# Attention and feed-forward on one core: the scale of x from the sums of squares of v, with a re-dealt instruction order

## The chip, the cores and the metric

The kernel runs on one core of a Trainium2 chip. The metric is device time in microseconds. The program before has a median of 1043.28 us over 3 runs (1041.65 to 1044.36).

## The reference, cut to what matters

```python
# q, k, v: (8 batches, 8 heads, 576 tokens, 64), float32
scores = (1 / sqrt(64)) * q @ k.transpose(0, 1, 3, 2)
scores = where(block_i >= block_j, scores, -1e9)      # blocks of 64 tokens, causal by block
attn = softmax(scores)
x = (attn @ v).transpose(0, 2, 1, 3).reshape(4608, 512)
h = x @ w_in                                          # 512 -> 2048
g = maximum(0.01 * h, h)
out = g @ w_out                                       # 2048 -> 512
```

Every row of `attn` sums to one, so a row of `x` is a weighted mean of rows of `v`.

## The kernel before, in words

**The work.** There are 64 pairs of batch and head ("heads" below) and 19 chunks of tokens, 256 tokens each except two of 128. Attention makes `x` head by head. The feed-forward layer takes a chunk when all eight heads have filled its tokens. Both are interleaved on TensorE, so that feed-forward matmuls (first layer L994, second layer L1012) stand between the attention steps of the later heads.

**One head of attention.** Scores go into the PSUM tile `p_s`: by matmuls in float32 for the first batch and the first part of the second (L586), with split operands `kk` and `qs` for the second and third (L603 and L598), with float16 operands from batch 3 on (L592). VectorE masks (L614) and takes the negated row maximum `nm` (L623). ScalarE takes the exponentials and their sums (L640). Both PSUM banks of `p_s` are used again by the next scores, so these wait until the exponentials have read them. Each head has two rounds: query tiles 0 to 3 (exponentials over 448, 64, 192 and 320 keys), then tile 4 over 576 keys. The sums are inverted (`rec`, L655 to L659). The probabilities are split into a float16 head (L682 on GpSimd, L683 on ScalarE, L684 on VectorE) and the rest (L687 on VectorE). A DMA transposes both (L694); TensorE multiplies them by the split `v` (L813), and L772 to L776 put the result, scaled back, into `x`. The tile of `x` is `xr`, which the profile calls `xr` for even and `slab` for odd batches; `slab` also holds the probabilities.

**Scales.** Operands of float16 matmuls are scaled by powers of two from their size. For `v`, `v_group` loads four heads at a time, takes their squares on ScalarE with an accumulator output (L882, one column of `vn` for each group), sums over partitions by a matmul with ones (L884), halves the exponent (`halved`, L399) and makes the scale and its inverse by integer arithmetic on the exponent (`powers`, L394 and L395). For q and k, `q_group` does the same with 40 squares from batch 3 on (L912, behind the loads `raw<-in_qk` at L911). For `x`, `scale_x` does it for each of ten groups of chunks that become ready together: it squares the tokens of these chunks on ScalarE (L948, a separate instruction for each batch and each half of the channels, 30 in all), adds the columns of `xn` (L958), sums over partitions (L959), and makes the scale `xs` and its inverse `xi`. `split_x` multiplies by `xs` and splits `x` into `xh` and `xl` (L973 to L977); the last layer's output is multiplied by `xi` (L1027).

**The feed-forward layer.** `ffn1` makes `p_h` (L994), ScalarE takes it to `g` (L999), `g` is cast to `gh` (L269 on ScalarE or L270 on VectorE), and the rest `gl` is subtracted on VectorE (L279) or GpSimd (L280). `ffn2` multiplies both by the output weights (L1012).

**What sets the order.** Each step is put into a `Plan` with a rank, what it reads and writes, and one or more engines with a cost for each. `Plan.run` steps through a model of the five engines: an engine that is free takes the ready step of the lowest rank, and a step that several engines can do goes to the first that takes it. The order found this way is written out for each engine, and the engine keeps it. Ranks are positions in units of one head plus an offset for each kind of step (`RL` for loads, `RP`, `RN`, `RV`, `RX` for the steps of a head, `RS` for the scale of `x` and its split, `VD`, `RQ` and `RD` for the groups of v and q). All DMAs stand in one queue, SyncE's.

Of the kernel before, what the change touches and what calls it, by code (L numbers as in the profile page):

```python
# [11 lines left out]
I32 = mybir.dt.int32  # L12
# [3 lines left out]
ALU = mybir.AluOpType  # L16
AX = mybir.AxisListType
# [5 lines left out]
S = 576  # L23
# [14 lines left out]
GROUP = 4  # L38
AHEADV = 3
AHEADQ = 5  # L40
RW = -0.559

RL = 4.551
RP = -0.707
RB = 0.386
RT = 1.718
RV = 2.066
RX = -5.319
RN = -1.998

LEAD = 4.4
LAG = 1.993
RS = 3.252
RG = 0.186
OFF1 = 3.425
OFF2 = -1.79
SL1 = 16.01
AHEAD = 0.432

LAT = 1550  # L60
HOLDP = 521.844
HOLD = 212.637
FILL = 235
FILLTO = 12
# [10 lines left out]
TOP = 204 << 23  # L75
# [2 lines left out]
SLOW = 8000  # L78
SIDE = 34
STEPA = 0.521  # L80
STEPB = 0.346
VD = 4.884
JOINT = 0
SB = 3
RQ = 3.568
RD = 1.25


class Plan:
# [161 lines left out]
def attention_ffn(ctx: ExitStack, tc: tile.TileContext, qk0: bass.AP, qk: bass.AP, v: bass.AP, w_in: bass.AP, w_out: bass.AP, out: bass.AP):  # L251
# [137 lines left out]
    qk16 = [carve(y, [4, S], F16) for y in range(2)]  # L389
    prow = [prow, [carve(1, [pw[t]], F32) for t in range(NT)]]  # L390

    def powers(e, s, i):
        return [
            lambda: nc.vector.tensor_scalar(s().bitcast(I32), e(), -1.0, float(TOP), op0=ALU.mult, op1=ALU.add),  # L394
            lambda: nc.vector.tensor_scalar(i().bitcast(I32), e(), float(BOT), None, op0=ALU.add),  # L395
        ]

    def halved(e, total):
# [541 lines left out]

    def scale_x(e, c0, c1, rank):
        spans_ = list(regions(c0, c1))
        for k, (_, b, o, ln, keys) in enumerate(spans_):

            for y in range(2):

                def square(k=2 * k + y, b=b, o=o, ln=ln, y=y):
                    nc.scalar.activation(  # L948
                        junk[:, : 2 * ln].rearrange("p (a b) -> p a b", a=2), xr[b % 2][:, 2 * y : 2 * y + 2, o : o + ln],
                        AF.Square, accum_out=xn[:, 4 * e + k : 4 * e + k + 1],  # L950
                    )

                near = [x for x in keys if x[2] // 4 == y]
                add([("ACT", act(2 * ln, True) + 190, square)], rank, near, [("xn", e, 2 * k + y), "junk"])
        x = bank()
        num = 2 * len(spans_)
        one = slice(e, e + 1)
        add([("DVE+", 75, lambda: nc.vector.tensor_reduce(xt[:, one], xn[:, 4 * e : 4 * e + num], axis=AX.X, op=ALU.add))], rank, [("xn", e, k) for k in range(num)], [("xt", e)])  # L958
        add([("PE", [(200, lambda: nc.tensor.matmul(p_t[x][:, 0:1], ones, xt[:, one], start=True, stop=True))])], rank, [("xt", e)], [("t", x)])  # L959
        add([("DVE", 68, lambda: halved(xe[:, one], p_t[x][:, 0:1]))], rank, [("t", x)], [("xe", e)])  # L960
        first, second = powers(lambda: xe[:, one], lambda: xs[:, one], lambda: xi[:, one])
        add([("DVE+", 68, first)], rank, [("xe", e)], [("xs", e)])
        add([("DVE+", 68, second)], rank, [("xe", e)], [("xi", e)])
        add([("DVE+", 68, lambda: nc.vector.tensor_mul(xi[:, one], xi[:, one], both))], rank, ["both"], [("xi", e)])
# [80 lines left out]
    for i in range(len(work) + 1):  # L1045
        if i == 0:

            def second(y):
                nc.gpsimd.memset(parts[y], 0.0)

            for y in range(2):
                new = [("ph", y, t, k) for t in (*range(NT), 6) for k in (0, 1)] + [("pt", y, t) for t in (*range(NT), 6)]
                new += [("p", 1, t) for t in range(NT)] + [(a, 1, d) for a in ("xh", "xl") for d in range(0, CH, BLK)] if y else [("x", 1, h, k) for h in range(H) for k in range(3)] + [("ob", 1)]
                new += [("x", y, k, "q") for k in range(4)]
                kind = "wo" if y else "wi"
                add([("POOL", 3300, lambda y=y: second(y))], 0, [("val", bool(y), f) for f in range(NF)], new)
        if i in events:
            here = [c for c in range(NCHUNK) if ready[c] == i]
            at = pos[i]
            nxt = pos[events[events.index(i) + 1]] if i != events[-1] else at + H  # L1060
            num = sum(sizes[c] for c in here) * NU
            done_ = 0
            e = events.index(i)
            scale_x(e, here[0], here[-1] + 1, at + LEAD - RS)
            for c, u in ((c, u) for c in here for u in range(NU)):
                rank = at + LEAD + (nxt - at) * done_ / num
                done_ += sizes[c]
                if u == 0:
                    split_x(c, e, rank - RS)
                ffn1(c, u, rank)  # L1070
                ffn2(c, e, u, rank + (nxt - at) * LAG * sizes[c] / num + 0.003)
        n, kind = work[i + AHEADV] if i + AHEADV < len(work) else (0, "")
        if kind in ("first", "full") and n % GROUP == 0:
            v_group((n - H) // GROUP)
        n, kind = work[i + AHEADQ] if i + AHEADQ < len(work) else (0, "")
        if kind == "full" and n >= SB * H and n % GROUP == 0:
            q_group((n - SB * H) // GROUP)
        if i < len(work):
            attention(i)
# [42 lines left out]
```

## Time and profile before

| | before |
|---|---|
| median of 3 runs | 1043.28 us |
| the profiled execution, whole time | 1045.07 us |
| its span from the first to the last instruction | 1043.3 us |
| TensorE clock granted in it | 1.000 |
| VectorE, ScalarE, GpSimd busy | 719.1, 723.0, 122.7 us |

The profile is of one execution, which took 1045.07 us, 1.79 us (0.17%) over the median of the runs shown; 1.8 us of it lie outside the span. In the views, PE is TensorE's matmuls, PEld its weight loads, DVE VectorE, ACT ScalarE, POOL GpSimd and SPq the queue in which SyncE issues DMAs. Times in the timeline count from the start of the span.

### The profile page before, as it was taken

The page shows a single profiled execution, that of the slowest core. Times are in us where ns is not written, and L with a number is a line of the kernel's source. Part 1 is how long each engine was busy: PE and PEld are TensorE (multiplying, and loading weights), DVE is VectorE, ACT ScalarE, POOL GpSimd, SP SyncE. Part 2 cuts the span into 40 slices and gives each one's busy share as a digit, 9 for nine tenths or more (in the row PEclk, how much of TensorE's full clock was granted, in tenths as well). Part 3 has the DMA queues.
Part 4 walks back from the last instruction along what each step waited for, and adds up shares of the span by engine and source line. Part 5 has one row for each costly group of instructions (what it writes and reads, how often), then busy time and mean ns, then how long its engine had stood idle before and what let it go on. Part 6 is the DMA issues. An engine that isn't in the chain of part 4 may idle for free. (4 is left out here: it accounts for less than half of the span.)

```text
span 1043.3 us, 22412 instructions
## 1 busy us (share of the span) xinstructions
PE 1023.5 (98%) x8496; PEld 740.3 (71%) x8496; DVE 719.1 (69%) x1942; ACT 723.0 (69%) x1692; POOL 122.7 (12%) x168
## 2 busy tenths in 40 slices
PE   9999999998999999999999999999999999999998
PEld 7787767776677777776767777777766777666665
DVE  4787788897888987898787878886666666221111
ACT  5788878778886887887787968786565666322222
POOL 1010122103130111100211101110100001000000
PEclk9999999999999999999999999999999999999999
DMA  7847456996987798989789889986736345100000
GB/s 259 278 164 245 147 137 139 204 195 135 226 183 160 185 219 168 205 188 220 152 167 186 200 189 185 178 184 121 137 92 149 80 98 85 29 1 21 21 1 31
DMA packets 266380, 155.54 MB, mean 149 GB/s; under 512 B 224288, under 2 KB 243232, under 8 KB 266272
## 3 DMA queue, kind: packets, MB, share of 16 engines
q1 hardware_dynamic: 266272, 154.11, 64.6%
q8 instruction: 66, 1.08, 0.4%
q14 instruction: 42, 0.34, 0.1%
HBM read 80.74 MB, written 9.44 MB: 86 GB/s over the span
## 5 line engine op out<-in xcount | busy, mean ns | idle before, releaser
L994 PEld LDWEIGHTS <-wih 128*128 128x128 f16 x2432 | 230.1, 98 | 67.1 <-issue 0.2
L999 ACT ACTIVATE g<-p_h 128x512 f32<-128x512 f32 (+1 forms) x152 | 86.5, 570 | 165.4 <-PE p_h L994 163.3
L994 PE MATMUL p_h<-slab,wih 128*128 128x256 f16 x1152 | 196.4, 273 | 0.0
L279 DVE TENSOR_TENSOR gl<-g,gh 128x512 bf16<-128x512 f32 (+1 forms) x118 | 77.9, 660 | 138.0 <-ACT gh L269 137.4
L1012 PE MATMUL p_o<-woh,gh 128*128 128x512 f16 x576 | 171.4, 379 | 0.0
L1012 PE MATMUL p_o<-wol,gh 128*128 128x512 f16 x576 | 171.3, 379 | 0.0
L1012 PE MATMUL p_o<-woh,gl 128*128 128x512 f16 x576 | 171.3, 379 | 0.0
L1012 PEld LDWEIGHTS <-gh 128*128 128x128 f16 x1152 | 109.7, 99 | 79.0
L994 PE MATMUL p_h<-xh,wih 128*128 128x256 f16 (+1 forms) x640 | 162.0, 262 | 0.0
L994 PE MATMUL p_h<-xh,wil 128*128 128x256 f16 (+1 forms) x640 | 161.9, 262 | 0.0
L994 PE MATMUL p_h<-xl,wih 128*128 128x256 f16 (+1 forms) x640 | 161.9, 262 | 0.0
L994 PE MATMUL p_h<-slab,wil 128*128 128x256 f16 x576 | 157.0, 273 | 0.0
L623 DVE TENSOR_REDUCE nm<-p_s 128x1 f32<-128x192 f32 (+4 forms) x308 | 138.2, 484 | 5.9 <-ACT prow L640 2.5
L994 PEld LDWEIGHTS <-wil 128*128 128x128 f16 x1216 | 118.9, 98 | 12.4
L1012 PEld LDWEIGHTS <-gl 128*128 128x128 bf16 x576 | 56.3, 98 | 67.9
L813 PEld LDWEIGHTS <-vs 128*128 128x128 f16 x1680 | 87.0, 98 | 12.8 <-issue 5.8
L813 PE MATMUL p_t<-slab,vs 128*128 128x128 f16 (+1 forms) x1680 | 90.2, 210 | 5.3 <-DMA slab<-slab 4.4
L687 DVE SCALAR_TENSOR_TENSOR slab<-prow,rec,slab 64x64 f16<-64x64 f32 (+4 forms) x148 | 79.0, 552 | 4.5 <-ACT slab L683 3.7
L687 DVE SCALAR_TENSOR_TENSOR slab<-slab,rec 128x448 f16<-128x448 f32 (+4 forms) x132 | 72.8, 575 | 1.4 <-ACT slab L683 1.0
L269 ACT CAST gh<-g 128x512 f16<-128x512 f32 (+1 forms) x120 | 71.4, 595 | 2.7
L280 POOL TENSOR_TENSOR gl<-g,gh 128x512 bf16<-128x512 f32 (+1 forms) x34 | 41.4, 1219 | 264.1 <-ACT gh L269 177.8
L592 PE MATMUL p_s<-slab 128*128 128x448 f16 (+2 forms) x480 | 67.6, 277 | 1.6 <-ACT prow L640 1.1
(165 smaller groups left out, 1497.7 us busy)
## 6 DMA issues: line engine op xcount, KB each, us to landing
qk_in<-in_qk SPq DMA_DIRECT2D x56, 576.0 KB, 4.9
raw<-in_qk SPq DMA_DIRECT2D x40, 288.0 KB, 3.8
slab<-slab SPq DMA_DIRECT2D x120, 72.0 KB, 4.4
raw<-in_w_in SPq DMA_DIRECT2D x16, 512.0 KB, 5.0
raw<-in_w_out SPq DMA_DIRECT2D x16, 512.0 KB, 4.3
out<-ob SPq DMA_DIRECT2D x19, 256.0 KB, 2.4
v_raw<-in_v SPq DMA_DIRECT2D x7, 640.0 KB, 4.8
raw<-in_v SPq DMA_DIRECT2D x7, 640.0 KB, 5.9
```

The costliest lines, as they stand in the source:

```text
L269: one = lambda: nc.scalar.copy(dst(), src())
L279: ("DVE+" if sb else "DVE", dve(n) + 100, lambda: nc.vector.tensor_sub(dst(), one(), two())),
L280: ("POOL", pool2(n) - (0.25 * n if n == 512 else 0), lambda: nc.gpsimd.tensor_sub(dst(), one(), two())),
L592: go = lambda ap=ap, cols=cols, k0=k0, k1=k1, c=c, first=first, last=last: nc.tensor.matmul(ap, sx1[:, cols], (sx3 if c else sx2)[:, k0:k1 ...
L623: [("DVE", dve(kw[t]), lambda t=t, ap=ap, flat=flat: nc.vector.tensor_reduce(nm[z][: qn[t], t : t + 1], ap[: qn[t]], axis=AX.X if flat els ...
L687: ("DVE+", dve(w) + 62, lambda: nc.vector.scalar_tensor_tensor(part(1), p, by, part(0), op0=ALU.mult, op1=ALU.subtract)),
L813: nc.tensor.matmul(p_t[x][:, c : c + src.free_size()], vs[z][:, (j + 1) % NT], src, start=start, stop=stop)
L994: nc.tensor.matmul(hh[:, i, :n], w[:, f, d, :], x[:, d, :n], start=k == 0, stop=k == len(terms) - 1)
L999: add([("ACT", act(2 * n), lambda: nc.scalar.activation(g[z][:, :, :n], hh[:, :, :n], AF.Prelu, alpha=0.01, scale=DOWN))], rank, [("h", z) ...
L1012: nc.tensor.matmul(p_o[m], a[:, i, m * P : (m + 1) * P], w[:, 2 * u + i, :], start=u == 0 and k == 0, stop=u == NU - 1 and k == 5,)
```

## The change

Two edits come together.

**The scale.** For a group of chunks that holds no token of batch 0, `scale_x` makes no squares of `x` any more. It reduces the columns of `vn` for the v groups of the batches that the chunks touch, and goes on as before, with an exponent that is 15 higher in `powers`, as `x` is kept 2^15 times too large (`UP`). Seven of the ten groups of chunks are such. The three others, two of batch 0 alone and one that spans batches 0 and 1, keep their 8 squares; 22 of the 30 squares and their accumulator reads go. The scale no longer depends on `x`, and its rank is lowered by a further `RX2` = 3.58 heads.

**The order.** Nineteen numbers are changed, which set the ranks and how long GpSimd holds back from a step, and `RX2` is new. The rest of the program is the same, but steps stand elsewhere, and some are on another engine: of the 152 subtractions that make `gl`, 46 are on GpSimd and not 34; GpSimd has 200 rows and not 173, VectorE 40 rows fewer, ScalarE 3 rows fewer. TensorE has the same matmuls in the same number.

```diff
-RS = 3.252
+RS = 3.835
...
-VD = 4.884
+VD = 5.061
...
-RD = 1.25
+RD = 1.347
+RX2 = 3.58
...
-    def powers(e, s, i):
+    def powers(e, s, i, more=0):
         return [
-            lambda: nc.vector.tensor_scalar(s().bitcast(I32), e(), -1.0, float(TOP), op0=ALU.mult, op1=ALU.add),
-            lambda: nc.vector.tensor_scalar(i().bitcast(I32), e(), float(BOT), None, op0=ALU.add),
+            lambda: nc.vector.tensor_scalar(s().bitcast(I32), e(), -1.0, float(TOP - (more << 23)), op0=ALU.mult, op1=ALU.add),
+            lambda: nc.vector.tensor_scalar(i().bitcast(I32), e(), float(BOT + (more << 23)), None, op0=ALU.add),
         ]
...
         spans_ = list(regions(c0, c1))
-        for k, (_, b, o, ln, keys) in enumerate(spans_):
+        b0, b1 = spans_[0][1], spans_[-1][1]
+        groups = range((b0 - 1) * H // GROUP, b1 * H // GROUP)
+        for k, (_, b, o, ln, keys) in enumerate(spans_ if not b0 else ()):
...
-        add([("DVE+", 75, lambda: nc.vector.tensor_reduce(xt[:, one], xn[:, 4 * e : 4 * e + num], axis=AX.X, op=ALU.add))], rank, [("xn", e, k) for k in range(num)], [("xt", e)])
+        each = vn[:, groups[0] : groups[-1] + 1] if b0 else xn[:, 4 * e : 4 * e + num]
+        add([("DVE+", 75, lambda: nc.vector.tensor_reduce(xt[:, one], each, axis=AX.X, op=ALU.add))], rank, [("vn", k) for k in groups] if b0 else [("xn", e, k) for k in range(num)], [("xt", e)])
...
-        first, second = powers(lambda: xe[:, one], lambda: xs[:, one], lambda: xi[:, one])
+        first, second = powers(lambda: xe[:, one], lambda: xs[:, one], lambda: xi[:, one], 15 if b0 else 0)
...
-            scale_x(e, here[0], here[-1] + 1, at + LEAD - RS)
+            scale_x(e, here[0], here[-1] + 1, at + LEAD - RS - (RX2 if begins[here[0]] >= S else 0))
```

Two places on ScalarE show what the order does. Lines of the changed kernel stand 1 further from L395 on, 4 further from L959 on.

**First place: a head of batch 2, whose exponentials of the first round run at 247 us in the trace of before.** `prow` and `slab` hold the probabilities of alternate heads, `junk,xn` is a square of x, `junk,vn` one of v, `junk,ptf` one of q. Before:

```order
L948 ACTIVATE junk,xn<-slab_78 128x768
L882 ACTIVATE junk,vn<-raw 128x1280
L640 ACTIVATE slab_79,sums_104<-p_s,nm_102 128x448
L912 ACTIVATE junk,ptf<-raw 128x576
L640 ACTIVATE slab_79,sums_104<-p_s,nm_102 64x64
L912 ACTIVATE junk,ptf<-raw 128x576
L640 ACTIVATE slab_79,sums_104<-p_s,nm_102 128x192
L912 ACTIVATE junk,ptf<-raw 128x576
L640 ACTIVATE slab_79,sums_104<-p_s,nm_102 128x320
L999 ACTIVATE g_142<-p_h_138 128x512
```

And now, for the same head:

```order
L684 ACTIVATE slab_78<-prow_84,rec_105 128x576
L641 ACTIVATE slab_79,sums_104<-p_s,nm_102 128x448
L641 ACTIVATE slab_79,sums_104<-p_s,nm_102 64x64
L641 ACTIVATE slab_79,sums_104<-p_s,nm_102 128x192
L641 ACTIVATE slab_79,sums_104<-p_s,nm_102 128x320
L1003 ACTIVATE g_141<-p_h_137 128x512
L270 CAST gh_149<-g_141 128x512
```

The square of x is gone, and the squares of v and q no longer stand between the exponentials of this head; they stand around those of the head before it, one v and one q square ahead of its four exponentials, three q squares behind them.

**Second place: a head of batch 4, whose exponential over 576 keys runs at 488 us in the trace of before.** Before:

```order
L272 ACTIVATE slab_78<-qk_in_93,ptf 128x576
L912 ACTIVATE junk,ptf<-raw 128x576
L999 ACTIVATE g_141<-p_h_137 128x512
L272 ACTIVATE slab_78<-qk_in_93,ptf 64x576
L640 ACTIVATE prow_84,sums_103<-p_s,nm_101,ptf 128x576
L948 ACTIVATE junk,xn<-slab_78 128x256
L655 ACTIVATE rec_105<-sums_103 128x1
L948 ACTIVATE junk,xn<-slab_78 128x256
L683 ACTIVATE slab_78<-prow_84,rec_105 128x576
```

And now:

```order
L1003 ACTIVATE g_141<-p_h_137 128x512
L913 ACTIVATE junk,ptf<-raw 128x576
L270 CAST gh_145<-g_141 128x512
L634 ACTIVATE nm_101<-nm_101,ptf 128x1
L273 ACTIVATE slab_78<-qk_in_93,ptf 128x576
L641 ACTIVATE prow_84,sums_103<-p_s,nm_101,ptf 128x576
L656 ACTIVATE rec_105<-sums_103 128x1
L684 ACTIVATE slab_78<-prow_84,rec_105 128x576
```

The two squares of x between the exponential and the split of its result are gone, and the square of q stands four steps ahead of the exponential, where it stood three ahead; one of the two copies of the next head's operands between them is no longer on ScalarE.

## The prediction on record

> **What bounds the kernel now.** The page comes first: who is busy, and which engine the chain that ended last runs over.
>
> ```profile
> PE 1023.5 (98%) x8496; PEld 740.3 (71%) x8496; DVE 719.1 (69%) x1942; ACT 723.0 (69%) x1692; POOL 122.7 (12%) x168
> PE 48%; DVE 0%; ACT 0%; issue 0%
> ```
>
> TensorE bounds the kernel. The change leaves its matmuls alone, so only its idle time can be won: 1043.3 - 1023.5 = 19.8 us. The view of busy time by stage, cut where the idle time changes, shows where that lies (columns: window, its length, then busy time and instructions of PE, PEld, DVE, ACT, POOL; clock; DMA).
>
> ```profile
> 0.00:130.00 130.00, 126.37 (x921) 100.83 (x922) 93.75 (x256) 104.96 (x256) 12.77 (x32) 1.00 0.67 219
> 130.00:240.00 110.00, 107.86 (x860) 76.98 (x859) 94.34 (x256) 85.31 (x207) 19.28 (x24) 1.00 0.75 164
> 240.00:300.00 60.00, 54.89 (x470) 40.66 (x468) 50.76 (x134) 51.51 (x125) 16.44 (x17) 1.00 0.81 181
> 300.00:480.00 180.00, 177.33 (x1657) 129.39 (x1655) 155.51 (x442) 146.14 (x350) 23.75 (x31) 1.00 0.87 189
> 480.00:500.00 20.00, 18.23 (x148) 12.51 (x146) 15.38 (x44) 15.02 (x42) 3.23 (x4) 1.00 0.99 228
> 500.00:560.00 60.00, 59.63 (x531) 43.18 (x529) 49.64 (x140) 47.08 (x109) 10.26 (x14) 1.00 0.85 176
> 560.00:1040.00 480.00, 479.17 (x3925) 336.75 (x3922) 259.69 (x676) 272.96 (x610) 37.01 (x47) 1.00 0.49 101
> ```
>
> PE idles 3.63 us before 130, then 2.14, 5.11, 2.67, 1.77 and 0.37 us up to 560, and 0.83 us in the 480 us after that. TensorE's order is the same in both kernels up to about 130 us, so the first stage stays. What is at stake is the middle: 2.14 + 5.11 + 2.67 + 1.77 + 0.37 = 12.06 us. The list of waits says what PE waited for (total, times, longest):
>
> ```profile
> PE p_t L813 <- DMA slab<-slab: 4.4, 7, 1.9
> PE p_s L603 <- ACT prow L640: 2.4, 2, 1.3
> PE p_s L586 <- ACT rec L655: 1.2, 2, 1.1
> PE p_s L603 <- ACT slab L640: 1.2, 2, 0.6
> PE p_s L592 <- ACT prow L640: 1.1, 2, 0.8
> ```
>
> So PE waits at the attention steps: for the transposed probabilities (4.4 us), and for ScalarE to have read the scores out of PSUM (2.4 + 1.2 + 1.1, and 1.2 us for the first part of batch 1). The list, which goes down to 0.5 us, has no second-layer matmul that waits for `gl`, and no first-layer matmul that waits for a split of x: the scale of x has cover. The change pays, if at all, through ScalarE's load and through the order.
>
> **The squares that go.** The stage view again, for L948 alone (busy us and instructions on ScalarE):
>
> ```profile
> 240.00:300.00 60.00, 2.07 (x4) 1.00 0.81 181
> 300.00:480.00 180.00, 4.03 (x10) 1.00 0.87 189
> 480.00:500.00 20.00, 1.95 (x6) 1.00 0.99 228
> 500.00:560.00 60.00, 0.92 (x2) 1.00 0.85 176
> 560.00:1040.00 480.00, 9.33 (x20) 1.00 0.49 101
> ```
>
> All of these go. The 9.33 us after 560 are worth nothing: PE is dense there, at ScalarE's 272.96 / 480 = 0.57 busy. Before 560 they are 2.07 + 4.03 + 1.95 + 0.92 = 8.97 us.
>
> What is ScalarE's relief worth to PE? The stages themselves give a curve. ScalarE's share against PE's idle share: 51.51/60 = 0.859 with 5.11/60 = 8.5%; 146.14/180 = 0.812 with 1.5%; 47.08/60 = 0.785 with 0.6%; 0.569 with 0.17%. The squares' time taken off, the shares become 0.824, 0.790, 0.769, and 0.654 for the short stage at 480. Read along straight lines between those points, idle becomes 3.3%, 0.8%, 0.6% and 0.35%, or 1.98, 1.39, 0.35 and 0.07 us: it falls by 3.13 + 1.28 + 0.02 + 1.70 = 6.1 us. I leave the stage from 130 to 240 out, since one removed square there is 1 us of 85. This is the upper end.
>
> The lower end is 0: no square of x stands in the chain of the three longest waits. Around 488 us ScalarE's row reads (last column: idle before, and what ended it)
>
> ```profile
> 486.35 0.68 ACT L912 ACTIVATE junk<-raw 128x576 bf16<-128x576 f32 x1 [1.18 <-DMA raw<-in_qk]
> 488.17 0.82 ACT L640 ACTIVATE prow<-p_s,nm,ptf 128x576 f32<-128x576 f32 x1
> 488.98 0.41 ACT L948 ACTIVATE junk<-slab 128x256 bf16<-128x256 f32 x1
> 489.93 0.76 ACT L683 ACTIVATE slab<-prow,rec 128x576 f16<-128x576 f32 x1
> ```
>
> and PE's, with the longest wait of all, at 254 us, as its third row:
>
> ```profile
> 489.13 1.03 PE L592 MATMUL p_s<-slab 128*128 128x448 f16 x8 [0.79 <-ACT prow L640]
> 491.15 1.57 PE L813 MATMUL p_t<-slab,vs 128*128 128x64 f16 x30 [0.99 <-DMA slab<-slab]
> 254.06 1.57 PE L813 MATMUL p_t<-slab,vs 128*128 128x64 f16 x30 [1.88 <-DMA slab<-slab]
> ```
>
> The wait of 0.79 is for an exponential behind a q square, which itself stood 1.18 us waiting for its load; the squares of x come after it. For the transposes, the median from issue to landing and the rows before the wait at 254:
>
> ```profile
> slab<-slab SPq DMA_TRANSPOSE x120, 4.7
> 243.98 0.78 ACT L683 ACTIVATE slab<-prow,rec 128x576 f16<-128x576 f32 x1 [0.30 <-DVE rec L659]
> 244.66 0.83 ACT L948 ACTIVATE junk<-slab 128x768 bf16<-128x768 f32 x1
> 247.87 2.14 SPq L694 DMA_TRANSPOSE slab<-slab  x1
> ```
>
> A transpose that lands at 491.1 was issued near 486.4, ahead of the squares at 488.98; and the one issued at 247.87 belongs to a split that ScalarE ended as the square at 244.66 began. Nor do the curve's stages differ in ScalarE's load alone: the one at 240 holds the subtractions of split operands (L279, L280), which end by batch 3. Between 0 and 6.1 us I take half, 3.0 us.
>
> **The scale's own steps.** Reduction, matmul with ones, exponent and inverse stay, ten times each; for seven of them the rank falls by RX2 = 3.58 heads and by the 0.58 that RS grows. Nothing of PE hangs on them now (no wait in the list above names a split or a scale), so I cost the move at nothing. What hides them is the chunk before, still in the feed-forward; without that cover each would cost about its own chain, a few short instructions.
>
> **The order.** The 12.06 us are dealt again. At 488 us the q square now stands a step further ahead of the exponential, which can give back up to 0.79. At 247 us three q squares and a v square no longer stand among a head's exponentials; this shortens that head's way to its transposes, and I set 1.0 us on it, about half of the 1.88. Together -1.8 us. The bounds: all of the idle time that the squares leave, 12.06 - 3.0 = 9 us, or, if the squares of v and q meet their loads and neighbours as badly one head earlier, a loss of 1.8.
>
> **GpSimd.** It has 27 instructions more, 12 of them subtractions for `gl`. Their prices, and one place where the two engines meet (columns of the first four rows: busy, mean ns, idle before):
>
> ```profile
> L279 DVE TENSOR_TENSOR gl<-g,gh 128x512 bf16<-128x512 f32 x106 | 72.8, 687 | 118.4 <-ACT gh L269 117.8
> L280 POOL TENSOR_TENSOR gl<-g,gh 128x512 bf16<-128x512 f32 x30 | 38.3, 1278 | 249.9 <-ACT gh L269 169.6 <-DVE gh L270 21.9 <-DVE rec L656 19.8
> L687 DVE SCALAR_TENSOR_TENSOR slab<-prow,rec,slab 128x448 f16<-128x448 f32 x28 | 19.5, 696 | 0.3
> L687 DVE SCALAR_TENSOR_TENSOR slab<-prow,rec,slab 64x64 f16<-64x64 f32 x32 | 10.8, 337 | 0.0
> 238.69 1.78 DVE L687 SCALAR_TENSOR_TENSOR slab<-prow,rec,slab 128x448 f16<-128x448 f32 x2
> 238.86 1.54 POOL L280 TENSOR_TENSOR gl<-g,gh 128x512 bf16<-128x512 f32 x1 [13.91 <-DVE slab L684]
> ```
>
> VectorE is relieved of 12 x 0.687 = 8.2 us. Against that, each `gl` on GpSimd comes 1.278 - 0.687 = 0.59 us later, and the two engines hold each other up: the pair of L687 at 238.69 took 1.78 us beside a GpSimd subtraction, where the means give 0.696 + 0.337 = 1.03, so 0.75 more. No second-layer matmul waited for `gl` by the list, so I take the delay of 0.59 as hidden by the matmuls that stand between a `gl` and its use. The holdup lies in the way to the transposes. If one in three of the 27 meets such an L687, it is 9 x 0.75 = 6.8 us; if VectorE's relief tells as much, a gain of a few tenths. I take +0.5 us, near the second end, as VectorE's 8.2 us outweigh most of the first.
>
> The Trainium skill, page "SBUF — State Buffer", section "Who interferes with whom", says more: a GpSimd instruction and a VectorE instruction with two SBUF inputs exclude each other, and whoever comes second waits until the first is done. The trace agrees with 0.75 us at 238.69. By that rule alone, with a VectorE instruction arriving on average halfway through 1.278 us, 9 meetings would make an estimated 5.8 us, and the sum below would turn to +1.0 us.
>
> **The sum.** -3.0 - 1.8 + 0.5 = -4.3 us. The profiled execution took 1045.07 us in all, so it becomes 1040.8; the median of the runs shown is 1.79 us lower, so the forecast for the median is 1043.28 - 4.3 = 1039.0 us. A difference of 0.3%, 3.1 us, is about what a measurement of this kernel can tell from none: faster is below 1040.2, slower above 1046.4.
>
> **The rivals.** *The curve holds in full.* ScalarE's load is the cause of the idle time, and its fall gives 6.1 us, with the order's 1.8: 1043.28 - 7.9 = 1035.4. For it speaks that idle rises with ScalarE's share at each of the four points; against it, the three waits above that no square of x is part of.
>
> *The relief is hidden.* ScalarE itself idles in these stages (at 480 it is busy 15.02 of 20 us), the waits are set by latency from scores to transposes, and the new order trades old waits for new ones: 0 - 0 + 0.5, so 1043.8. For it speak the same three waits; against it, that four of the five listed kinds end on ScalarE, directly.
>
> *GpSimd holds VectorE up.* The 27 instructions meet the L687 on the way to the transposes: 6.8 us against the relief of 3.0, so 1043.28 + 3.8 = 1047.1. It decides the sign as soon as more than four of the meetings (3.0 / 0.75) lie where PE has no other work. For it speaks that PE's largest wait is for transposes; against it, that only 7 of the 120 transposes are waited for at all.
>
> **How the numbers follow.** The forecast has 0.47, the full curve 0.13, the hidden relief 0.27, GpSimd 0.13. A tenth of the forecast's 0.47 lies above 1040.2. Faster: 0.42 + 0.13 = 0.55; same: 0.27 + 0.05 = 0.32; slower: 0.13. The forecast's own range is 1036 to 1041. The full range goes down past the full curve towards the order's bound of 9 us, to 1032.0, and up to 1046.5, short of the GpSimd case, which leaves out some 0.05 below and 0.12 above.
>
> **What would show it.** Right: ScalarE's busy time is about 15 us or more lower, PE's idle from 240 to 560 falls from 9.9 us to 6 or less, and the wait at the scores for `prow` and `slab` of L640 shrinks most. The curve: idle from 300 to 480 falls under 1.4. Hidden: ScalarE's time falls, PE's idle doesn't. GpSimd: L687 and the wait for transposes (4.4 us now) grow, with GpSimd rows beside them. Wrong altogether: a wait of PE for `gl`, for a split of x, or any new one after 560 us.

## The result, and the profile after

The changed kernel takes 1055.53 us (median of 6 runs, 1052.67 to 1059.84); the kernel before took 1043.82 us beside it (6 runs, 1041.65 to 1048.57). The ratio is 1.0113, with a 95% interval of 1.0090 to 1.0135: 11.7 us slower, where 4.3 us faster was forecast. The profiled execution took 1054.29 us, with a span of 1052.3 us, 9.0 us longer than before's.

The page of the changed kernel, first the busy times, then what the chain that ended last runs over:

```profile
PE 1025.9 (97%) x8496; PEld 741.4 (70%) x8496; DVE 708.6 (67%) x1901; ACT 711.7 (68%) x1665; POOL 149.6 (14%) x195
PE 35%; DMA 1%; ACT 0%; issue 0%; SPq 0%; DVE 0%
```

ScalarE is 11.3 us less busy and VectorE 10.5, as the change meant. TensorE is 2.4 us more busy with the same matmuls, and idles 1052.3 - 1025.9 = 26.4 us, 6.6 more than before; 2.4 + 6.6 is the whole 9.0. The stages (columns as in the prediction; last but two the granted clock, last but one the busy share of the DMA engines):

```profile
0.00:130.00 130.00, 127.12 (x925) 101.15 (x926) 94.82 (x259) 106.05 (x258) 13.55 (x34) 1.00 0.67 219
130.00:240.00 110.00, 106.12 (x854) 75.85 (x853) 94.48 (x252) 82.86 (x209) 25.63 (x32) 1.00 0.76 164
240.00:300.00 60.00, 54.03 (x457) 39.25 (x455) 47.91 (x125) 44.61 (x112) 21.07 (x21) 1.00 0.83 184
300.00:480.00 180.00, 174.98 (x1615) 127.07 (x1614) 147.14 (x415) 140.59 (x337) 32.10 (x39) 1.00 0.87 182
480.00:500.00 20.00, 17.94 (x161) 13.44 (x159) 15.13 (x43) 14.40 (x36) 2.57 (x4) 0.92 1.05 224
500.00:560.00 60.00, 60.00 (x515) 43.37 (x514) 46.86 (x135) 46.23 (x108) 11.78 (x13) 1.00 0.84 179
560.00:1040.00 480.00, 477.44 (x3914) 336.22 (x3913) 261.03 (x676) 274.65 (x607) 42.90 (x54) 1.00 0.49 103
```

Read against before, TensorE idles 3.88 us from 130 to 240 (2.14), 5.97 to 300 (5.11), 5.02 to 480 (2.67), 2.06 to 500 (1.77), 0 to 560 (0.37) and 2.56 after that (0.83). From 130 to 500 and after 560 every stage loses, 0.3 to 2.4 us each; before 130 and from 500 to 560 none does. It comes where ScalarE got lighter: from 240 to 300 ScalarE fell from 51.51 to 44.61 us and the idle time rose by 0.86. The windows are cut by time, so a window holds somewhat other work after than before. The list of PE's waits:

```profile
PE p_t L814 <- DMA slab<-slab: 4.3, 5, 1.3
PE p_s L604 <- ACT slab L641: 3.7, 4, 1.5
PE p_s L604 <- ACT prow L641: 3.2, 2, 2.0
PE p_s L593 <- DMA slab<-slab: 3.0, 4, 1.2
PE p_s L587 <- ACT prow L641: 1.6, 1, 1.6
PE p_s L593 <- ACT prow L641: 1.3, 1, 1.3
```

Against before, the wait for transposes is the same (4.4), the waits for exponentials to clear the scores' banks grew from 2.4 + 1.2 + 1.1 to 3.7 + 3.2 + 1.6 + 1.3 us, and a kind that hardly stood there is new: 3.0 us (0.5 before) for the float16 operands of q and k, which three small DMAs complete (L550 to L552). So in this profile the growth stands at ScalarE (some 5 us) and at these copies (2.5), and none at the transposes. No matmul waits for `gl` or for a split of x; of the scale's steps only one is waited for, 0.3 us by the matmul at L885, until the exponent `xe` is taken.

The longest wait, from 243.5 to 245.55 us, as ScalarE's rows and then PE's show it:

```profile
242.60 0.68 ACT L913 ACTIVATE junk<-raw 128x576 bf16<-128x576 f32 x1 [1.43 <-DMA raw<-in_qk]
243.28 0.76 ACT L273 ACTIVATE kk<-qk_in,eighth 128x576 fp32r<-128x576 f32 x1
244.06 0.58 ACT L773 ACTIVATE slab<-p_t,vin 64x384 f32<-64x384 f32 x1
244.67 0.74 ACT L641 ACTIVATE prow<-p_s,nm 128x576 f32<-128x576 f32 x1
245.55 1.38 PE L604 MATMUL p_s<-kk,qs 128*128 128x448 f32 x8 [2.05 <-ACT prow L641]
```

A square of q (L913) stands ahead of the others in ScalarE's order and waits 1.43 us for its load; the exponential three rows behind it comes late, and the next scores wait 2.05 us for it. This is the place where the prediction saw the squares of q move "one head earlier". The second place repeats itself at 493 us, and there the clock comes in (PE's rows, and the window view):

```profile
494.62 1.03 PE L593 MATMUL p_s<-slab 128*128 128x448 f16 x8 [1.25 <-ACT prow L641]
496.46 2.62 PE L814 MATMUL p_t<-slab,vs 128*128 128x64 f16 x30 [0.81 <-DMA slab<-slab]
495.00:500.00 5.00, 4.19 (x42) 3.64 (x41) 2.68 (x8) 1.64 (x3) 0.23 (x1) 0.67 1.30 234
```

Two waits, 1.25 + 0.81 us within some 3 us, and the granted clock falls: the 30 matmuls take 2.62 us where the same row took 1.57 before. By the stage's clock of 0.92 this place makes 0.08 x 20 = 1.6 of the 2.4 us by which TensorE is busier.

And the operands of q and k, at 355 us, in SyncE's queue:

```profile
345.31 4.25 SPq L695 DMA_TRANSPOSE slab<-slab  x2
349.65 0.81 SPq L526 DMA_DIRECT2D qk_in<-in_qk  x1
350.56 0.47 SPq L550 DMA_DIRECT2D slab<-slab  x1
351.08 0.59 SPq L551 DMA_DIRECT2D slab<-slab  x1
351.72 0.59 SPq L552 DMA_DIRECT2D slab<-slab  x1
```

The rows of VectorE, which makes what the first and third copies move, and of TensorE, which reads all three:

```profile
345.90 0.80 DVE L547 SCALAR_TENSOR_TENSOR slab<-qk_in,ptf,slab 128x576 f16<-128x576 f32 x1
```
```profile
356.71 0.58 PE L593 MATMUL p_s<-slab 128*128 128x448 f16 x3 [1.18 <-DMA slab<-slab]
```

The wait ended with the second copy (L551). What it moves is read by L547 too, so it was ready by 345.90, and what the others move at 346.70; the copies were issued from 350.56 on, behind transposes and a load, the second at 351.08. It landed 5.6 us later, and the scores waited 1.18 us.

### The profile page after: what moved, and what is told of

Its sections match the earlier page's. It is cut to its first block, busy times and chain, and to the rows that moved or that the text cites. A ratio compares the mean times of both kernels' runs of the same rounds, so it can differ in the third digit from the quotient of the medians.

```text
span 1052.3 us, 22379 instructions
## 1 busy us (share of the span) xinstructions
PE 1025.9 (97%) x8496; PEld 741.4 (70%) x8496; DVE 708.6 (67%) x1901; ACT 711.7 (68%) x1665; POOL 149.6 (14%) x195
## 5 line engine op out<-in xcount | busy, mean ns | idle before, releaser
L280 DVE TENSOR_TENSOR gl<-g,gh 128x512 bf16<-128x512 f32 (+1 forms) x106 | 69.3, 654 | 145.6 <-ACT gh L270 131.6
L281 POOL TENSOR_TENSOR gl<-g,gh 128x512 bf16<-128x512 f32 (+1 forms) x46 | 57.2, 1243 | 245.2 <-ACT gh L270 205.3
L688 DVE SCALAR_TENSOR_TENSOR slab<-prow,rec,slab 128x576 f16<-128x576 f32 (+4 forms) x148 | 75.8, 535 | 3.4 <-ACT slab L684 3.1
L270 ACT CAST gh<-g 128x512 f16<-128x512 f32 (+1 forms) x127 | 75.2, 592 | 2.7
L688 DVE SCALAR_TENSOR_TENSOR slab<-slab,rec 128x448 f16<-128x448 f32 (+4 forms) x132 | 70.1, 557 | 3.7 <-ACT slab L684 3.4
```

Of the source, the lines that this page charges most:

```text
L270: one = lambda: nc.scalar.copy(dst(), src())
L280: ("DVE+" if sb else "DVE", dve(n) + 100, lambda: nc.vector.tensor_sub(dst(), one(), two())),
L281: ("POOL", pool2(n) - (0.25 * n if n == 512 else 0), lambda: nc.gpsimd.tensor_sub(dst(), one(), two())),
L688: ("DVE+", dve(w) + 62, lambda: nc.vector.scalar_tensor_tensor(part(1), p, by, part(0), op0=ALU.mult, op1=ALU.subtract)),
```

## The experiments

Two theories stood at the start. A: the new order costs the time, and the squares are neutral or a gain. B: leaving the squares out, or taking the scale from `vn`, costs it. All times are medians; each ratio is to the kernel before on the same chip. Differences in the text are of medians, across chips too; by the ratios they come out up to 2 us otherwise, with the same signs.

| kernel | us | ratio, 95% interval |
|---|---|---|
| old order, squares out | 1043.58 | 0.9996, 0.9985 to 1.0007 |
| changed kernel, old numbers, RX2 = 0 | 1047.66 | 1.0039, 1.0026 to 1.0052 |
| the same, RX2 = 3.58 | 1048.19 | 1.0045, 1.0033 to 1.0057 |
| kernel before, new numbers | 1054.32 | 1.0112, 1.0094 to 1.0131 |
| kernel before, VD alone new | 1059.94 | 1.0163, 1.0141 to 1.0185 |
| changed kernel, VD alone old | 1057.98 | 1.0151, 1.0133 to 1.0169 |
| new order, fourth q squares later | 1065.28 | 1.0203, 1.0184 to 1.0222 |
| new order, these squares and a load later | 1059.34 | 1.0157, 1.0134 to 1.0179 |
| old order, squares of x out, the same | 1045.29 | 1.0023, 1.0012 to 1.0033 |
| new order, `gl` on VectorE | 1061.78 | 1.0165, 1.0144 to 1.0187 |
| new order, copies from ScalarE's queue | 1059.86 | 1.0150, 1.0130 to 1.0171 |
| new order, no q squares | 1056.41 | 1.0131, 1.0114 to 1.0148 |
| new order, no q squares, no q loads | 1046.25 | 1.0030, 1.0016 to 1.0043 |
| old order, no squares, no q loads | 1038.94 | 0.9951, 0.9936 to 0.9966 |
| new order, no transposes | 1040.46 | 0.9975, 0.9960 to 0.9991 |
| old order, squares of x out, no transposes | 1036.31 | 0.9935, 0.9914 to 0.9956 |
| new order, q loads from ScalarE's queue | 1085.68 | 1.0411, 1.0383 to 1.0438 |
| old order, squares of x out, the same | 1064.52 | 1.0215, 1.0192 to 1.0238 |

"Old order" and "new order" mean that every engine keeps the rows of the kernel before, or of the changed kernel, and only what is named is left out or put elsewhere.

### Squares or order

**The squares alone.** The planner still deals with the 22 squares, so that the order stays; they are only not issued, and the scale is taken from `vn` as in the changed kernel.

```diff
                 def square(k=2 * k + y, b=b, o=o, ln=ln, y=y):
+                    if b0:
+                        return
                     nc.scalar.activation(
...
```

> The kernel before with its order kept on every engine, row by row; only the 22 squares of x for chunks without batch 0 are not issued, and the scale comes from the columns of vn. Theory A (the new order costs the time, the squares are neutral or a gain): 1041 to 1044 us, no slower than before, TensorE's idle time from 130 to 560 us at most before's 12.06 us. By the curve of the prediction (idle time follows ScalarE's load) it would be 6 us faster, 1038. Theory B (taking the scale from vn or leaving the squares out itself costs time): 1050 us or more, slower than before by 6 us or more.

1043.58 us, the same as before to 0.1%. Theory B falls, and so does the gain. The stages of this kernel:

```profile
240.00:300.00 60.00, 55.67 (x460) 40.96 (x460) 51.54 (x136) 50.34 (x122) 15.97 (x16) 1.00 0.83 184
300.00:480.00 180.00, 177.04 (x1651) 128.92 (x1650) 154.98 (x440) 142.34 (x341) 23.99 (x31) 1.00 0.87 189
```

From 300 to 480 ScalarE is 3.8 us lighter than before (146.14) and TensorE idles 2.96 us, 0.3 more.

**The numbers alone, and parts of them.**

```diff
 changed kernel, planner without squares:   the 19 numbers of before, RX2 = 0.0  (then 3.58)
 kernel before, planner with squares:       the 19 new numbers
```

> The changed kernel with the nineteen numbers of before and RX2 = 0: the planner sees no squares of x and deals the order anew. Theory A as a cost of the new numbers: at the time of before, 1041 to 1046 us. Theory A as a lottery (any new deal of the order lands somewhere, by which waits it happens to make): anywhere from 1040 to 1060 us, and not tied to the numbers. Theory B: 1050 us or more, like the changed kernel's 1055.5.

> The same with RX2 = 3.58, so the scale's steps (reduction, matmul with ones, exponent) stand 3.58 heads earlier. If the early scale costs the time (its matmul with ones or its short VectorE steps get in the way of heads): 5 us or more above the kernel with RX2 = 0. If not: its time differs only as any other deal of the order does, within some 10 us of it either way.

> The kernel before, squares of x and all, with the nineteen new numbers. Theory A as a cost of the new numbers: slower than before by about 10 us, 1050 to 1058 us, as the changed kernel; the squares on top make it at most 3 us slower than that. Theory B: near before, 1041 to 1047 us.

The new numbers cost about as much with the squares (1054.32, 10.4 us) as without (1055.53, 11.7). The early scale costs nothing that can be told (1048.19 against 1047.66). But the old numbers without squares in the planner's list are 3.7 us slower too: a re-deal is enough. Two more deals, one number each:

```diff
 kernel before:    VD 4.884 -> 5.061
 changed kernel:   VD 5.061 -> 4.884
```

> The kernel before, squares and all, with one of the nineteen numbers changed to its new value: VD, the rank of v's groups, from 4.884 to 5.061. If the nineteen numbers of before are one good draw and nearly any other draw is worse (lottery): 1046 to 1056 us. If the loss needs the new numbers together: 1042 to 1046 us.

> The changed kernel, with VD alone set back from 5.061 to 4.884; the planner deals anew. VD alone cost the kernel before 16 us. If VD is what the loss hangs on: 1043 to 1048 us. If any deal falls somewhere, and the numbers don't add up: anywhere from 1046 to 1060.

One of the nineteen numbers alone costs 16 us, more than all nineteen and more than the lottery was given (1056); taken out of the nineteen it gives nothing back. So the numbers don't add up. Seven deals were measured, and the one of the kernel before is the fastest; whether it was picked from many is not for these runs to say. Theory A holds as a lottery: the order costs the time, and by which of its places is not shown by these runs.

### Single waits, or something behind them

Theory C: the new order is slow by a handful of waits that can be taken away one by one. Theory D: what is taken away comes back at the next step.

**The squares of q.** Three buffers hold the q that these squares read, so the fourth load of a group can only be issued when the first square is done, and its square is the one that waits at 242.6 and 491.6 us. It was moved behind the next exponential over 576 keys:

```diff
+        for fn in [f for f in order if getattr(f, "name", "") == "q3"]:
+            k = order.index(fn)
+            e = next(j for j in range(k, len(order)) if getattr(order[j], "name", "") == "e4")
+            order.insert(e, order.pop(k))
```

> The changed kernel in its own order, but the fourth square of q of each of the ten groups stands on ScalarE behind the next exponential over 576 keys and not ahead of it. Theory C (the new order is slow by a handful of waits that can be named, among them two squares of q that wait for their load ahead of an exponential, at 242.6 and 491.6 us): the waits of 2.0 and 1.3 us at the scores go and with them the drop of the clock at 497 us, which is worth some 1.7 us; 3 to 5 us faster than the changed kernel, 1050.5 to 1052.5 us. Theory D (the waits are latency of the whole attention path, and what is taken away at one place comes back at the next): 1054 to 1056 us.

1065.28 us, 9.8 over the changed kernel, but this misses its aim: the square had now passed a load into its own buffer, so it took another head's sum and waited for that load (2.55 us at 245.54). In the next kernel that load moves with it, in SyncE's queue:

```diff
...
+            moved = [j for j in range(k, e) if names[j] in (("q", one), ("load", one + 3))]
...
```

> The changed kernel in its own order, but the fourth q square of each group stands on ScalarE behind the next exponential over 576 keys, and a load that fills the same buffer again and would have come between is moved behind it in SyncE's queue. (In the kernel with the squares alone moved, the square came behind that load, read the wrong head and waited for it: 2.55 us at 245.54.) Theory C (single waits that can be named and taken away): the waits of 2.0 at 243 and 1.3 at 493 us go, 3 to 5 us faster than the changed kernel, 1050.5 to 1052.5. Theory D (what is taken away at one place comes back at the next, since heads, queue and buffers hang together): the wait at 243 goes, but the total stays within 2 us of the changed kernel, 1053.5 to 1057.5.

1059.34 us, 3.8 slower than the changed kernel. The two waits for `prow` that it was to remove are gone; in the list of waits, and in PE's rows, stands instead

```profile
PE p_t L826 <- DMA slab<-slab: 9.9, 8, 3.0
PE p_s L616 <- ACT slab L653: 4.7, 4, 2.4
```
```profile
499.07 1.12 PE L826 MATMUL p_t<-slab,vs 128*128 128x64 f16 x21 [2.99 <-DMA slab<-slab]
```

The wait for transposes went from 4.3 to 9.9 us: at 496 to 499 us the second product waits 2.99 us, where the changed kernel had 1.25 for scores and 0.81 for transposes. Done to the old order, it costs 1.7 us:

> The kernel before in its own order without the 22 squares of x (1043.6 us), and with the fourth q square of each group and its buffer's next load moved behind the next exponential over 576 keys. Theory C: the wait of 0.79 us at 489 us goes, 0.5 to 2 us faster, 1041.5 to 1043. Theory D: within 1 us of 1043.6 or slower.

Then the 40 squares were left out altogether, loads kept (`sn` set to a constant, so the scales of q and k are constants):

```diff
             def blocks():
+                nc.gpsimd.memset(sn, 576.0)
...
-            add([("ACT", act(S, True) + 190, lambda buf=buf, one=one: nc.scalar.activation(
+            add([("ACT", act(S, True) + 190, lambda buf=buf, one=one: None if one >= 0 else nc.scalar.activation(
                 junk[:, :S], buf, AF.Square, accum_out=sn[:, one : one + 1]
```

> The changed kernel in its own order, with the 40 squares of q not computed and their sums set to a constant, so the scales of q and k from batch 3 on are constants; loads and all else stay. This takes the waits of the q squares for their loads off ScalarE altogether and 40 x 0.87 = 35 us of its work. Theory C: at least 4 us faster than the changed kernel, 1051.5 or less; if ScalarE's load at large sets TensorE's idle time (the curve of the prediction), 6 us or more, below 1049.5. Theory D: 1052.5 to 1056.

1056.41 us. ScalarE is 26.9 us less busy than in the changed kernel, and nothing is won. The waits again:

```profile
PE p_t L814 <- DMA slab<-slab: 9.9, 9, 2.8
PE p_s L593 <- DMA slab<-slab: 4.1, 4, 1.2
PE p_s L604 <- ACT slab L641: 3.6, 4, 1.3
```

Scores wait less for ScalarE (3.6 and 1.2 us for L604, where it was 3.7 and 3.2), and what they win, TensorE stands at DMAs, 14.0 us for the two kinds and not 7.3. Theory C falls: what is taken away does not come off the time. D had that right; the times are above its ranges all the same, here and in the three other kernels of this part that have one, by 0.4 to 9.3 us.

**GpSimd.** The 46 subtractions for `gl` go to VectorE, at their places:

```diff
-nc.gpsimd.tensor_sub(dst(), one(), two())
+(nc.vector if n >= 256 and first == "POOL" else nc.gpsimd).tensor_sub(dst(), one(), two())
```

> The changed kernel in its own order, but all 46 subtractions for gl that it has on GpSimd are on VectorE, at the same place of the program. GpSimd theory (GpSimd's subtractions hold up VectorE on the way to the transposes): 4 us or more faster than the changed kernel, 1051 us or less. Theory C: none of the named waits is for GpSimd; VectorE gains 46 x 0.69 = 32 us of work, so between 1 us faster and 4 us slower, 1054 to 1059.5 us.

1061.78 us, 6.3 slower than the changed kernel, so in this order they are better off on GpSimd. What they cost the way to the transposes there is small: VectorE's 280 subtractions on it (L688) took 75.8 + 70.1 = 145.9 us in the changed kernel and 75.2 + 69.1 = 144.3 us here. Here too the wait for transposes is what grew most:

```profile
PE p_t L814 <- DMA slab<-slab: 8.7, 12, 1.5
```

**The copies' place in the queue.**

```diff
-nc.sync.dma_start(sx1[64:128], sx4[64:128])      (and the two other copies)
+nc.scalar.dma_start(sx1[64:128], sx4[64:128])
```

> The changed kernel in its own order, but the three copies of the split q and k of each head from batch 3 on are issued from ScalarE's DMA queue and not from SyncE's, where they stand behind the transposes. Theory C: PE's waits of 3.0 us in all for these copies go, with up to 1.5 us lost again where ScalarE issues 120 DMAs; 1052 to 1055 us. Theory D: the copies share the DMA engines with the transposes anyhow, and the wait stays at 2 to 3 us; 1055 to 1058 us.

1059.86 us. The wait for the copies is gone from the list, and the transposes took its place:

```profile
PE p_t L814 <- DMA slab<-slab: 8.8, 7, 2.4
```

### The DMA side

Each time the wait for transposes grew. From 130 to 560 us the DMA engines are busy 76 to 105% by the stages above, so the DMA theory says that they are a second bound, against a chain theory (TensorE's order and the way from scores to transposes cost it, whatever else the queue carries). Two things were left out, each in both orders: the 40 q loads of 288 KB with their squares, and the 120 transposes (their tile set to zero once, so that the output is zero).

```diff
...
-lambda buf=buf, k=k: nc.sync.dma_start(buf, qk[b - 1, h + k][:, 0])
+lambda buf=buf, k=k, e=e: None if e >= 0 else nc.sync.dma_start(buf, qk[b - 1, h + k][:, 0])
```

> The changed kernel in its own order with neither the 40 squares of q nor the 40 loads of 288 KB that only these read; their scales are constants. DMA theory (the transposes come late because SyncE's queue and the DMA engines are full): 4 us or more below the kernel without the squares alone (1056.4), 1052.5 or less. Chain theory (the order of TensorE and the way from scores to transposes cost it, whatever else the queue carries): 1054.5 to 1057.

> The kernel before in its own order without the squares of x (1043.6), without the squares of q and without their loads. DMA theory: 1 to 3 us faster, as there are fewer waits for transposes to win (4.4 us): 1040.5 to 1042.5. Chain theory: 1042.5 to 1044.5.

```diff
             def turn():
+                if e > a:
+                    return
                 nc.sync.dma_start_transpose(turned[y2][:, a:e, :], parts[y2][:, a:e].rearrange("p a k -> p (a k)"))
...
```

> The changed kernel in its own order with the 120 DMA transposes left out; the tile that they fill is set to zero once, so the output is zero and TensorE's second product waits for no DMA. DMA theory: the waits for transposes (4.3 us) and for the copies (3.0 us) go, and with them most of what the new order lost: 1044 to 1048 us. Chain theory: only the 4.3 us go, and waits at the scores take some of it back: 1049 to 1053 us, still 8 us or more above the old order without transposes.

> The kernel before in its own order without squares of x and without the 120 DMA transposes, output zero. Both theories: the 4.4 us of waits for transposes go, 1038 to 1041 us. What tells is the distance to the new order without transposes: 5 us or less by the DMA theory, 8 us or more by the chain theory.

Without the loads the new order gains 10.2 us on the kernel without the squares alone (1046.25 against 1056.41), where the squares themselves had given nothing; the old order, whose squares were not left out by themselves, gains 4.6. Without transposes the two orders take 1040.46 and 1036.31 us. The distance of new to old is 1055.53 - 1043.58 = 12.0 us in full, 7.3 us without squares and loads of q, and 4.2 us without transposes. Leaving out the transposes does two things at once, though: the DMA engines carry less, and TensorE's second product waits for no exponential and no split any more. How much of the 15.1 us that it gives the new order is the one or the other is not shown; the loads of q feed only the squares, which gave nothing by themselves.

For the 4.2 us that stay the lists of waits give a hint. Without transposes the scores wait for ScalarE 8.2 us in the new order and 4.1 in the old; with them it was 10.7 in the changed kernel and 5.9 in the kernel before. The profiled execution of the old order without transposes lies 3.9 us above its median, so this is no more than a hint. The longest of these waits, new order first:

```profile
PE p_s L604 <- ACT slab L641: 4.3, 4, 2.1
PE p_s L587 <- ACT prow L641: 1.8, 1, 1.8
```
```profile
PE p_s L603 <- ACT prow L640: 2.4, 2, 1.3
PE p_s L603 <- ACT slab L640: 1.5, 2, 0.9
```

The stage from 300 to 480 in four kernels, in this order: new order without q squares, without q loads too, old order without q loads, new order without transposes:

```profile
300.00:480.00 180.00, 172.42 (x1594) 125.15 (x1595) 143.67 (x406) 131.06 (x311) 31.83 (x39) 1.00 0.87 180
```
```profile
300.00:480.00 180.00, 176.49 (x1648) 128.42 (x1646) 148.23 (x419) 132.63 (x315) 32.70 (x40) 1.00 0.79 164
```
```profile
300.00:480.00 180.00, 177.25 (x1658) 129.47 (x1656) 155.49 (x445) 132.98 (x314) 24.00 (x31) 1.00 0.82 170
```
```profile
300.00:480.00 180.00, 178.69 (x1672) 131.08 (x1670) 151.19 (x428) 144.62 (x349) 34.00 (x41) 1.00 0.37 110
```

With ScalarE at the same 131 to 133 us, TensorE's idle time goes from 7.58 to 3.51 us as the DMA share goes from 0.87 to 0.79, and to 1.31 at 0.37, with ScalarE at 144.62. Within the new order it follows the DMAs and not ScalarE. The share alone does not set it: in the old order the same 0.87 goes with 2.67 us of idle time (kernel before) and 2.96 (squares of x out). Three of the four sizes were larger than the DMA theory had said (1044 to 1048 for the new order without transposes, 1040.5 to 1042.5 and 1038 to 1041 for the two old ones); the signs, the 1052.5 or less and the distance of 5 us or less came as it said. The chain theory's ranges were missed by all four.

Is it the traffic, or the loads' place ahead of transposes in SyncE's queue? The loads were issued from ScalarE's queue instead, all work kept.

```diff
-nc.sync.dma_start(buf, qk[b - 1, h + k][:, 0])
+nc.scalar.dma_start(buf, qk[b - 1, h + k][:, 0])
```

> The changed kernel in its own order, complete, with the 40 q loads issued from ScalarE's DMA queue and not from SyncE's. Queue theory (they cost by standing ahead of transposes in SyncE's queue, and waiting there for a buffer): 4 us or more faster than the changed kernel, 1046 to 1051.5. Traffic theory (they cost by what they move): 1053 to 1059, no gain, as with the copies of q and k (1059.9).

> The kernel before in its own order without the 22 squares of x (1043.6), complete, with the 40 q loads issued from ScalarE's DMA queue. Queue theory: 2 to 4 us faster, 1039.5 to 1041.5, which would beat both kernels. Traffic theory: 1043 to 1046.

1085.68 and 1064.52 us: 30 and 21 us slower. Neither theory had that; the queue theory falls as it was put, and the traffic theory lacked a piece. What the transposes do, in the old order, first the kernel before, then with the loads in the other queue (issue to landing in 240 to 560 us, shortest, median, longest), and PE's wait there:

```profile
DMA to landing us min/median/max: 3.6/4.8/7.5
```
```profile
DMA to landing us min/median/max: 3.6/4.7/10.2
```
```profile
PE p_t L813 <- DMA slab<-slab: 17.3, 9, 5.7
```

Half of the transposes land as before, but the longest takes 10.2 us and not 7.5 (14.5 and not 8.4 in the new order), and PE's waits for them go from 4.4 to 17.3 us. One place shows how. In the old order with all in one queue a transpose is issued at 246.83 us, the loads of q follow from 248.81 on, the transpose lands 5.7 us after its issue and the second product waits 1.29 us. With two queues the same transpose is issued at 246.79, loads stand in the other queue at 247.46, 248.41 and 249.60, the transpose lands after 9.5 us, and PE's row reads

```profile
256.33 1.86 PE L813 MATMUL p_t<-slab,vs 128*128 128x64 f16 x20 [5.12 <-DMA slab<-slab]
```

So the load no longer stands behind the transpose's issue, and the transpose, for which TensorE waits, pays. With the copies in the other queue the median rose too, from 5.1 to 5.9 us in the new order. The Trainium skill, page "DMA: Bandwidth & Descriptors", section "Queues, rings and completion order", says that each DMA engine takes turns between the queues for which it has work; the longer landings agree with that. Of the 25.6 us by which the span of the new order grew, 18.0 are more waits for transposes (22.3 and not 4.3) and 7.2 a busier TensorE (1033.1 and not 1025.9, at a granted clock of 0.95 from 300 to 480). What ScalarE's part in issuing 40 loads (its rows show 0.33 us each) adds to the waits was not taken apart.

No complete kernel here beats the kernel before clear of the noise. Of the three clearly below it two have no transposes, and the one at 1038.94 us has constants for the scales of q and k.

## Why the prediction was wrong

**What bounds it, and where.** TensorE bounds the kernel, the last stage is worth nothing to win, and the waits lie at scores and transposes: right. That only the 12.06 us of idle time from 130 to 560 were at stake was half of it: this is what can be won, not what can be lost. The idle time there became 16.9 us, 1.7 us came from 560 to 1040, and TensorE's busy time, taken as fixed, grew by 2.4.

**The squares, -3.0 us.** Failed. Measured alone they are worth 0.4 us with an interval of 1.1 us to either side. The curve of idle time against ScalarE's share was four stages in which the DMA share differed too (0.81, 0.87, 0.85 and 0.49 in the rows that the prediction quoted, a column it did not use). Two stages of the same table lie off it: from 480 to 500 TensorE idles 8.9% with ScalarE at 15.02 / 20 = 0.75, where the curve has 0.5% (1.70 of its 6.1 us came from there), and from 130 to 240 it idles 1.9% at 85.31 / 110 = 0.78. So "idle rises with ScalarE's share at each of the four points" was true of the points picked. Taking 26.9 us more off ScalarE gave nothing. The lower end, argued from the chain of single waits, was the right one.

**The scale's own steps, nothing.** Right: 0.3 us of waits for them after, and 1048.19 against 1047.66 us with RX2 alone.

**The order, -1.8 us, with -9 to +1.8.** This is the step that failed: 12 us the other way. The prediction gave 0.79 and 1.0 us for two places as if the rest of the order stood still. At both places its own bad case came, a q square that meets its load (1.43 us at 242.60, 1.40 at 491.61), and it was priced at 1.8 us, what the two places had been hoped to give. But the order was dealt anew everywhere, ScalarE keeping little over half of its rows in their sequence (some 740 of 1280 by the two traces), and five other deals were 3.7 to 16 us slower as well. So the term that was -1.8 us measured some +12 us, 1055.53 against 1043.58, outside both of its bounds. A new deal that is worse should have been the rival on the slow side.

**GpSimd, +0.5 us.** Not measured alone: all 46 subtractions were moved, not the 12 that the change added. The sign named for the GpSimd rival did not come. With 27 instructions more on GpSimd, VectorE's L687 (L688 after) went from 79.0 + 72.8 = 151.8 us down to 145.9, and the wait for transposes stayed at 4.3; with no `gl` on GpSimd, L688 gets only 1.6 us shorter. So 6.8 us for the meetings is not borne out, nor the estimate of 5.8 us by the Trainium skill's rule on shared access to SBUF, which took nine of them. That two engines exclude each other at one place is not touched by this.

**The signs named beforehand.** ScalarE's busy time fell by 11.3 and not by 15, since other steps came to it; the idle time from 240 to 560 rose from 9.9 to 13.1 us; the wait at the scores, which was to shrink most, grew most; and new waits came after 560 (1.3 us for transposes, 1.1 for the copies), the sign of "wrong altogether".

**The rivals.** "The relief is hidden" is right for the squares, and it saw that new waits replace old ones, but it put the order at nothing. The GpSimd case had the sign, by a cause that did not show, so that is luck. None of the three had the new order as a loss of its own. Shown is that the order costs the 12 us and the squares nothing, that in the new order the loads of q cost 10 us where their squares cost none, and that each of four repairs came back as a longer wait for transposes. Argued from this is that DMAs needed at set times, through one queue, on DMA engines that are nearly full, carry most of the loss: its two thirds (12.0 to 4.2 us) that go with the transposes may in part be the way over ScalarE and VectorE that goes with them. What in the new order makes the steps meet worse stays open.

## What to carry to other kernels

Price a removal and a re-dealt order apart, and for the second ask first how many steps change places: if nearly half of them do, as here, the two places that one can read say little, and the slow side needs a wide range. Before an engine's load is taken for the cause of idle time, read the DMA column beside it, ask what else differs between the stages of such a curve, and look at the stages that it leaves out. When a wait is removed, look where the consumer stands next: in none of the three kernels that took the waits of single steps away here (q squares and a load moved, q squares out, copies moved) did the time fall.

## What was not expected of the hardware

Moving 40 loads to a second queue made some of the transposes that stayed slower: a longest landing of 14.5 us instead of 8.4, with the median at 5.3 and not 5.1, and 30 us in the whole.

The clock fell without a long pause. From 493 to 497 us TensorE stood for 1.25 and 0.81 us, after some 480 us of nearly dense work, and the granted clock was 0.67 from 495 to 500. One pause of 2.05 us at 243 us left it at 1.00 from 240 to 250, so neither the longest pause nor the sum of pauses decides alone; what does was not measured. The Trainium skill, page "TensorE: Matmul & The Clock Gate", section "HAM oscillation — how this bites in real kernels", gives the rule as no pause over some 3.4 us; the trace differs: it shows the drop with pauses of 2.06 us in sum, none over 1.25, so here shorter pauses, close together, go with it.
